# Top-k attention with an MLP behind it: two MLP pieces between two steps' scores, and an earlier place for the weights' transposing read

## The chip, the cores and the metric

One core of one Trainium2 chip runs the whole program. The metric is the device time of one execution in microseconds (us); lower is better. In the profile PE is TensorE's matrix multiply, PEld its weight load, DVE is VectorE, ACT is ScalarE, POOL is GpSimd, and SP is SyncE, which here only issues DMAs.

## What is computed

The attention takes 8 batches of 8 heads, 576 positions and 64 dimensions, and keeps the 32 largest scores of each row. Its output, as 4608 rows of 512, goes through a two-layer MLP.

```python
scores = scale * np.matmul(q, k.transpose(0, 1, 3, 2))
kth = np.partition(scores, -top_k, axis=-1)[..., -top_k:-top_k + 1]
scores = np.where(scores >= kth, scores, -1000000000.0)
attn = softmax(scores)                   # max subtracted, sum + 1e-09
x = np.matmul(attn, v)                   # then (B,H,S,D) -> (B*S, H*D)
h = x @ w_in                             # 4608x512 @ 512x2048
g = np.where(h >= 1, h, np.where(h <= -1, 0, (h + 1) ** 2 / 4))
out = g @ w_out                          # 2048x512
```

## The kernel before

**Steps.** The attention is cut into 144 steps (`n = len(steps)`). A step is one tile of 128 query rows for two heads; four steps make one chunk of 128 complete rows of x, and there are 36 chunks. Two batches share one chunk made of their last 64 rows. A step goes through these stages, which belong to different engines:

- `scores` (L349): matmuls on TensorE into two PSUM tiles `sp` (tag "a", 2 buffers), copied by ScalarE to `s` in two halves (L368). There are four `s` tiles.
- `weights` (L426) on VectorE: the search for the 32nd largest value (L381 to L460), then the masking of the exponentials `e` with their sum (L467). ScalarE makes `nmax` and `e` (L402, L404) from the first maxima. `divide` takes the reciprocal on VectorE (L413), and GpSimd scales `e` with it (L420), in the next step.
- `move_w` (L493): ScalarE splits `e` into 16-bit `halves` (L497), SyncE writes them to a DRAM tile `rows`, and a transposing DMA reads them back as `wT`. The read is put on the list `reads_of_rows` and issued later. Steps 0 to 7, and the last two, transpose on TensorE instead (`transpose_w`, L482).
- `values` (L506): `wT` with v on TensorE into `po` (tag "ph", 3 buffers), copied by ScalarE to `xT` (L527).

**The MLP in pieces.** When the fourth step of a chunk has its values, `mlp` (L538) adds 24 pieces to the queue `pending`. Eight are hidden pieces, called h0 to h7 here, of cost 8; sixteen are final pieces, f0 to f15, of cost 4; a chunk is 128 units. A hidden piece multiplies xT by w_in into a PSUM tile `ph` (tag "ph" too). Its `read` (L554) is two ScalarE activations, into `r` (2 buffers) and `g` (L558, L566), and its `bound` (L572) is three GpSimd instructions on r and g (L573, L575, L576). A final piece multiplies g by w_out into `py` (1 buffer); after f15, ScalarE copies `py` to `y` (L589) and SyncE stores it. The last eight final pieces of a chunk are marked, and are set among the next chunk's first hidden pieces.

**The order.** Everything is issued in the order of the program text (`manual_schedule`), so each engine's queue has that order. Each step of the loop (L801) has seven places (`slot` 0 to 6). The relevant ones are these:

- place 0: the first part of `weights`; the waiting transposing reads are issued.
- place 1: `queries(m + 5)` and one part of the next batch's key preparation. For batch 1 (`keys_of`, steps 8 to 11 here) a part is four TensorE transposes out of `k_in` (1 buffer), two ScalarE copies, and the load of the next `k_in`; at step 10 it also loads that batch's v. For later batches (`turned_keys_of`, at even steps) a part is a ScalarE copy into `parts` (L287), a write and a transposing read.
- place 2, at even steps: scores of step m + 2, then `issue_reads`, then the two values that are due (`values_until((m - 2) // 2 * 2)`), then scores of step m + 3.
- place 3: `inspect` at odd steps (L173: ScalarE looks at a `raw` piece of the MLP's weights, loaded by SyncE), `move_w` of step m - 1, then the loads that wait in `loads`.

At the end of each place `advance` takes pieces from `pending`. It keeps a credit, `due`:

```python
            due = due + amount if pending else 0.0
            pe_time = max(pe_time, until - 4.0)
            while pending and due >= pending[0][0] and pe_time < until and take():
                pass
```

`take` subtracts the piece's cost from `due` and adds it to `spent`. The amount per place is a seventh of `share`, which is what is left of the whole MLP over the steps left, but no more than what is pending over the steps until the next chunk comes.

In places 1 and 2 of even steps `holding` is set: the `read` of a hidden piece taken there is kept in the list `reads` and issued by `issue_reads` behind the scores of step m + 2. Anywhere else the read follows its matmuls at once:

```python
                reads.append(partial(read, x, ph))
                if not holding:
                    issue_reads()
```

Steps up to 7 are "early": the weights of the MLP are still being converted, and values are issued one step behind. At step 8 the loop issues values 7 with the old rule (L850), so at steps 8 and 10 no values are due in place 2; the first pair is values 8 and 9 at step 12.

Of the kernel before, what the change touches and what calls it, by code (L numbers as in the profile page):

```python
# [26 lines left out]
def kernel(  # L27
# [18 lines left out]
    NHP = H // 2  # L46
# [130 lines left out]
    def run(ctx, paired):  # L177
# [116 lines left out]
        def issue(x):  # L294
            while x:
                x.pop(0)()
# [235 lines left out]
        def rows_of(b, t):  # L532
            r0 = b * S
            if t < NT:
                return [(0, P, out[r0:r0 + SM, :].rearrange("(p c) n -> p c n", c=NT)[:, t, :])]
            return [(i * TL, (i + 1) * TL, out[r0 + i * S + SM:r0 + (i + 1) * S, :]) for i in range(2)]
# [110 lines left out]
        n = len(steps)  # L647
# [6 lines left out]
        pending = deque()  # L654
# [5 lines left out]
        def issue_reads():  # L660
            while reads:
                reads.pop(0)()
# [3 lines left out]
        def convert(time):  # L666

            nonlocal converted, begun
            while begun < min(converted + (2 if paired else 1), n_pieces):
                pipe.append(convert_piece(words, begun, not paired))  # L670
                next(pipe[-1])
                begun += 1
            next(pipe.popleft())
            converted += 1
            usable[converted] = time
            for i in range(begun, converted + (len(room) or 2)):
                load(words, i)
# [13 lines left out]
        def take():  # L691

            nonlocal spent, due, pe_time, taken
            cost, pieces, work, _ = pending[0]
            if pieces > converted or usable[pieces] > pe_time + 0.5:
                return False
            pending.popleft()
            due -= cost
            spent += cost
            pe_time += cost * UNIT_TIME  # L700
            work()
            taken = work.func
            return True

        def advance(amount, until):

            nonlocal due, pe_time
# [4 lines that stand above are left out]
            due = min(due, 24.0)  # L712
# [74 lines left out]
        next_keys, valued = 1, 0  # L787

        def values_until(m):
            nonlocal valued, pe_time  # L790
            while valued < min(m, n):
                pe_time = max(pe_time, ready_at[valued]) + 1.25
                values(state[valued])
                state[valued] = None
                if valued in ready:
                    ch = ready[valued]
                    mlp(xTs[ch], rows_of(*chunks[ch]), mlp_pool, ch == len(chunks) - 1)
                valued += 1

        first_late = None  # L800
        for m in range(n + 2):  # L801
            early = converted < n_pieces
            if not early and first_late is None:
                first_late = m
            elif not early and late is None:
                conversion.close()
                room.clear()
                late = ctx.enter_context(tc.tile_pool(name="late", bufs=1))

            share, left = (total - spent) / (n + 2 - m), sum(x[0] for x in pending)  # L810
            for r in sorted(ready):
                if r + 4 > m and r >= valued:
                    share = min(share, left / (r + 4 - m))
                    left += NK * NF + NF * DM // P
            top_k, parts = None, [0] * SLOTS
            if m < n:
                top_k = weights(state[m], state[m - 1] if m > 0 else None, state[m + 1] if m + 1 < n else None)
                parts = [1] * SLOTS if early else [1, 1, 0, 1, 1, 1, 1]
                start = max(dve_time, scored[m])
                now_converting = range(0, SLOTS, 2)  # L820
                dve_time = start + K_TIME + PIECE_TIME * min(len(now_converting), n_pieces - converted)
                done[m] = dve_time
                state[m]["by_tensor"] = early or m >= n - 2
            for slot in range(SLOTS):
                now = start + (dve_time - start) * (slot + 1) / SLOTS
                for _ in range(parts[slot]):
                    next(top_k, None)
                if slot == 0 or m >= n - 3:
                    issue(reads_of_rows)
                if m < n and converted < n_pieces:  # L830
                    if slot in now_converting:
                        convert(now)
                elif slot == 3 and late is not None:
                    if m % 2:
                        inspect()
                if slot == 1 and 1 <= m <= n and state[m - 1]["by_tensor"]:
                    pe_time = max(pe_time, done[m - 1] + 2.0) + 1.0
                    transpose_w(state[m - 1])
                    ready_at[m - 1] = pe_time + 1.8
                if slot == 3 and 1 <= m <= n and state[m - 1] is not None and not state[m - 1]["by_tensor"]:  # L840
                    move_w(state[m - 1])
                    ready_at[m - 1] = done[m - 1] + 15.0
                if slot == 1 and late is not None and paired and m % 2 == 0:
                    load(late, inspected, 1, 2)
                if slot == 3:
                    issue(turns)
                    issue(loads)
                if slot == SLOTS - 1 and m == n + 1 and paired:
                    judge(ps, att)
                if slot == 2 and (early or m == first_late or m >= n - 1):  # L850
                    values_until(m)
                if m == 0 and slot in (1, 2):
                    next(first)
                holding = not early and m % 2 == 0 and slot in (1, 2) and m < n
                if slot == 2 and not early:
                    if m % 2 == 0:
                        while len(reads) < 3 and pending and taken is not None and taken.__name__ == "hidden" and take():
                            pass
                    begin_until(min(m + 2, len(state)))
                    holding = False  # L860
                    issue_reads()
                    values_until((m - 2) // 2 * 2)
                    begin_until(m + 3 - m % 2)
                if slot == 4 and early:
                    begin_at(m + 2)
                if slot == (6 if early else 1):
                    queries(m + (3 if early else 5))
                    if (m < n and prep is None and next_keys < B and steps[m][0] == next_keys - 1 and steps[m][1] >= 1
                            and (next_keys > 1 or converted == n_pieces)):
                        prep = (turned_keys_of if next_keys > 1 else keys_of)(next_keys)  # L870
                    if prep is not None and (m % 2 == 0 or next_keys == 1):
                        got = next(prep, None)
                        pe_time += 0.5 if next_keys < 2 else 0.0
                        if got is None:
                            prep, next_keys = None, next_keys + 1
                        else:
                            keys[next_keys] = got
                            value_loads = got.get("loads", value_loads)
                    elif value_loads is not None:
                        loads.append(partial(next, value_loads, None))  # L880
                if paired and early and spent == 0 and not pending:
                    rest = ps.tile([P, NT, P], F32, name="rest", tag="py", bufs=1)
                    for i in range(5):
                        nc.tensor.transpose(rest[:, i % NT, :], ident, ident)  # L884
                advance((EARLY_SHARE if early else share) / SLOTS if m < n - 2 else 32.0, now)
                slots_done += 1
                while bounds and (early or m >= n or bounds[0][0] < slots_done - 2):
                    bounds.popleft()[1]()
            for _ in (top_k if top_k is not None else ()):
                pass  # L890
# [52 lines left out]
```

## Time and profile before

| what | value |
|---|---|
| median of 3 runs | 1472.83 us (1472.76 to 1473.66) |
| the profiled execution | 1471.88 us, its span 1470.1 us |
| mean granted TensorE clock | 0.992 |
| busy share of the span: PE, DVE, ACT, POOL | 97%, 95%, 79%, 63% |
| transposing reads of `rows` | 134, and as many writes of 576 KB, 3.2 us to landing |
| TensorE's scores of steps 18 and 142 start at | 196.41 and 1370.6 us |

The span is what the profiler saw from the first to the last instruction; the execution's own time is 1.8 us more. Busy shares are means over stages that differ. In the rows of groups and waits, a line such as L547 is the line of the code above, the count behind x is the number of instructions, and the name behind an arrow is what ended a wait.

### The profile page before, as it was taken

To read this page: it belongs to the slowest core of one execution; us is meant where nothing else is said; L and a number is where in the kernel's file an instruction comes from. 1 tells how busy PE (TensorE), PEld (TensorE's weight loads), DVE (VectorE), ACT (ScalarE), POOL (GpSimd) and SP (SyncE) were. 2 spreads that over 40 slices of the span, in tenths; PEclk is the share of its full clock that TensorE was granted. 3 is DMA by queue.
4 is the path that set the end of the run, shared out by engine and by line. 5 is a ranking of instruction groups with operands and counts; after the bars stand their busy time and mean duration, and the time that the engine had idled before them with its cause. 6 is when DMAs were issued, how large, how long until landed. Compare 5 with 4: busy or idle time off the path is not lost.

```text
span 1470.1 us, 32068 instructions
## 1 busy us (share of the span) xinstructions
PE 1433.2 (97%) x10787; PEld 1049.5 (71%) x10787; DVE 1395.7 (95%) x4392; ACT 1160.2 (79%) x2222; POOL 930.9 (63%) x1310
## 2 busy tenths in 40 slices
PE   6998899999999999999999999999999999999998
PEld 5776577777777777777777777777777777777777
DVE  6989999999999999999999999999999999999922
ACT  6986878888778888887778887888778888777642
POOL 3564577667666666666666666666666666666640
PEclk7999999999999999999999999999999999999999
DMA  7642766876778877886667797997667987665410
GB/s 233 199 133 57 201 161 183 217 188 165 164 177 211 217 200 192 210 218 177 173 168 204 207 216 177 224 215 181 174 165 187 224 214 175 167 163 151 137 41 17
DMA packets 508159, 260.42 MB, mean 177 GB/s; under 512 B 458704, under 2 KB 467152, under 8 KB 507984
## 3 DMA queue, kind: packets, MB, share of 16 engines
q1 hardware_dynamic: 507984, 258.27, 68.3%
q8 instruction: 87, 1.43, 0.4%
q14 instruction: 88, 0.72, 0.2%
HBM read 62.39 MB, written 102.63 MB: 112 GB/s over the span
## 4 chain that ended last, share of the span: by engine, by line
PE 91%; ACT 4%; DMA 2%; issue 1%; DVE 1%; SPq 1%; ACTq 0%
PE ph L547 34%; PE py L586 32%; PE sp L367 11%; PE po L514 10%; PE po L522 1%; PE pw L482 1%; DMA wT<-rows 1%; PE py_half L600 1%; ACT s L368 1%; ACT units L147 1%; ACT halves L497 1%; ACT wT L485 1%; ACT e L404 0%; DMA xT<-in_k_dram 0%; PE rest L884 0%
## 5 line engine op out<-in xcount | busy, mean ns | idle before, releaser
L547 PEld LDWEIGHTS ph<-xT,w_in 128*128 128x128 f32 x4608 | 547.0, 192 | 97.7 <-issue 66.8
L547 PE MATMUL ph<-xT,w_in 128*128 128x128 f32 x4608 | 555.6, 276 | 2.4 <-ACT g L566 1.8
L586 PE MATMUL py<-w_out,g 128*128 128x512 f32 x1120 | 526.6, 597 | 1.6 <-ACT y L589 1.6
L573 POOL TENSOR_SCALAR r<-r 128x256 f32<-128x256 f32 x280 | 138.3, 494 | 402.1 <-ACT r L558 397.9
L388 DVE MATCH_REPLACE8 more<-tops,more 128x288 f32<-128x288 f32 x864 | 379.1, 445 | 0.0
L420 POOL TENSOR_SCALAR e<-e,rz 128x576 f32<-128x576 f32 x268 | 304.3, 1145 | 12.6 <-DVE rz L413 12.6
L586 PEld LDWEIGHTS py<-w_out,g 128*128 128x128 f32 x1120 | 193.9, 191 | 164.9 <-issue 162.9
L497 ACT COPY halves<-e 128x1152 uint16<-128x1152 uint16 x268 | 293.8, 1144 | 0.0
L576 POOL TENSOR_TENSOR g<-r,g 128x256 f32<-128x256 f32 x280 | 233.4, 834 | 22.0
L467 DVE SCALAR_TENSOR_TENSOR e<-s,kth,e 128x577 f32<-128x577 f32 x288 | 242.9, 881 | 0.1
L404 ACT ACTIVATE e<-s,nmax 128x576 f32<-128x576 f32 x288 | 223.0, 775 | 4.7
L558 ACT ACTIVATE r<-ph,half 128x256 f32<-128x256 f32 (+1 forms) x296 | 136.9, 462 | 105.1 <-PE ph L547 100.5
L368 ACT ACTIVATE s<-sp 128x576 f32<-128x576 f32 x288 | 171.8, 650 | 43.2 <-PE sp L367 41.5
L575 POOL TENSOR_TENSOR r<-r 128x256 f32<-128x256 f32 x276 | 181.0, 656 | 23.0
L367 PE MATMUL sp<-kT,qT 64*128 64x288 f32 x1024 | 161.9, 434 | 4.8 <-ACT kT L265 3.4
L367 PEld LDWEIGHTS sp<-kT,qT 64*128 64x128 f32 x1024 | 89.8, 188 | 75.9 <-issue 30.5
L514 PE MATMUL po<-wT,v_in 128*64 128x128 f32 x2048 | 138.7, 276 | 4.9 <-DMA wT<-rows 4.1
L381 DVE TENSOR_TENSOR more<-s 128x576 f32<-128x576 f32 x144 | 134.7, 935 | 8.8 <-ACT s L368 8.8
L514 PEld LDWEIGHTS po<-wT,v_in 128*64 128x64 f32 x2048 | 113.4, 137 | 29.1 <-issue 12.2
L566 ACT ACTIVATE g<-ph,minus 128x256 f32<-128x256 f32 x280 | 130.8, 467 | 0.0
L429 DVE MAX8 tops<-more 128x8 f32<-128x288 f32 x288 | 125.9, 447 | 0.0
L437 DVE MAX8 tops<-more 128x8 f32<-128x288 f32 x288 | 117.0, 449 | 0.0
(95 smaller groups left out, 1370.1 us busy)
## 6 DMA issues: line engine op xcount, KB each, us to landing
rows<-halves SPq DMA_DIRECT2D x134, 576.0 KB, 3.2
lines<-parts SPq DMA_DIRECT2D x48, 256.0 KB, 3.3
q_in<-in_q_dram SPq DMA_DIRECT2D x32, 256.0 KB, 4.5
v_in<-in_v_dram SPq DMA_DIRECT2D x32, 256.0 KB, 4.0
raw<-in_moe_w_in_dram SPq DMA_DIRECT2D x32, 256.0 KB, 3.3
raw<-in_moe_w_out_dram SPq DMA_DIRECT2D x32, 256.0 KB, 3.2
out_dram<-y SPq DMA_DIRECT2D x31, 256.0 KB, 3.3
kT<-in_moe_w_in_dram SPq DMA_DIRECT2D x8, 512.0 KB, 4.5
```

Of the source, the lines that this page charges most:

```text
L367: nc.tensor.matmul(*x, start=True, stop=True)
L368: nc.scalar.activation(s[:, :, c0:c1], sp[:, :, 0:SH], AF.Copy, scale=SCALE)
L388: nc.vector.match_replace(out=st["rest"][:, i, :], in_to_replace=eight(st["tops"], i, r - 8), in_values=src[:, i, :], imm_value=LOWEST)
L404: nc.scalar.activation(e[:, i, :], s[:, i, :], AF.Exp, bias=nmax[:, i:i + 1])
L420: nc.gpsimd.tensor_scalar(st["e"][:, i, :], st["e"][:, i, :], rz[:, i:i + 1], 1.0, ALU.mult, ALU.mult)
L467: nc.vector.scalar_tensor_tensor(out=st["all"][1][:, i, :], in0=st["all"][0][:, i, :], scalar=last[i], in1=st["all"][1][:, i, :], op0=ALU. ...
L497: nc.scalar.copy(halves[:, :, i * S:(i + 1) * S], st["e"][:, i, :].bitcast(U16).rearrange("p (k t) -> p t k", t=2))
L514: nc.tensor.matmul(po[j * D:(j + 1) * D], v_in[:, h, c, :] if c < NT else tail_values(v_tl, h, t), wT[:, block(j, c)], start=(c == 0), sto ...
L547: nc.tensor.matmul(ph[:, i], w_in[:, kk, f * P:(f + 1) * P], xT[:, kk], start=(kk == 0), stop=(kk == NK - 1))
L575: nc.gpsimd.tensor_tensor(out=r, in0=r, in1=r, op=ALU.mult)
L576: nc.gpsimd.tensor_tensor(out=g, in0=r, in1=g, op=ALU.add)
L586: nc.tensor.matmul(py[0], gs[f // group][:, f % group], w_out[:, f, :], start=(f == 0), stop=(f == NF - 1))
```

## The change

It has two parts.

```diff
+        def fill(amount):
+            for _ in range(amount):
+                if pending:
+                    take()
+
...
-                if slot == 0 or m >= n - 3:
+                if slot == 0 or m >= n - 3 or slot == 5 and m < 4 * NHP:
                     issue(reads_of_rows)
...
                     begin_until(min(m + 2, len(state)))
                     holding = False
                     issue_reads()
+                    if valued >= (m - 2) // 2 * 2 and m % 2 == 0:
+                        fill(2)
                     values_until((m - 2) // 2 * 2)
                     begin_until(m + 3 - m % 2)
```

The first part: in place 2 of an even step, if the values that could be due there are already done, two pieces are taken from `pending` between the scores of step m + 2 and those of step m + 3. They are taken whatever the credit is; their cost goes from `due` all the same. With values issued as described above, the condition holds at steps 8, 10 and 144.

The second part: `NHP` is 4, so up to step 15 the transposing read of the step's `move_w` (place 3) is issued in place 5 of the same step, where before it was issued in place 0 of the next one. Since `move_w` starts with step 9, this concerns the reads of states 8 to 14.

## The prediction

> **What bounds the kernel now.** I read the page's busy shares, then busy time in stretches of 40 us, then the waits of TensorE, then SyncE's queue, then two steps instruction by instruction.
>
> ```profile
> PE 1433.2 (97%) x10787; PEld 1049.5 (71%) x10787; DVE 1395.7 (95%) x4392; ACT 1160.2 (79%) x2222; POOL 930.9 (63%) x1310
> ```
>
> In the stretches (columns: PE, PEld, DVE, ACT, POOL busy us) the gaps lie early:
>
> ```profile
> 120.00:160.00 40.00, 33.15 (x238) 23.98 (x236) 37.20 (x120) 30.27 (x62) 16.52 (x24) 0.96 0.42 122
> 160.00:200.00 40.00, 35.96 (x318) 27.11 (x322) 40.00 (x127) 32.30 (x63) 21.80 (x31) 1.00 0.69 183
> ...
> 1080.00:1120.00 40.00, 40.00 (x287) 28.99 (x286) 40.00 (x126) 30.88 (x61) 27.77 (x38) 1.00 0.64 168
> ```
>
> From 260 to 1400 us the list of waits holds none of TensorE's matmuls: four steps take it 37.77 us again and again. So TensorE sets the end; later than 260 us nothing is to be gained from it, and each new stall there is paid. TensorE's timeline shows the early gaps, in brackets with what ended them:
>
> ```profile
> 142.60 2.82 PE L547 MATMUL ph<-xT,w_in 128*128 128x128 f32 x16 [1.83 <-ACT g L566]
> ...
> 151.12 0.46 PE L341 MATMUL pq<-ident,q_tl 64*128 64x64 f32 x4 [1.25 <-ACT s L368]
> 152.38 0.63 PE L261 MATMUL pk<-ident,k_in 128*128 128x128 f32 x4 [0.80 <-DMA k_in<-in_k_dram]
> ...
> 162.45 1.09 PE L514 MATMUL po<-wT,v_in 128*64 128x128 f32 x16 [2.66 <-DMA wT<-rows]
> ...
> 195.39 1.10 PE L586 MATMUL py<-w_out,g 128*128 128x512 f32 x2 [1.60 <-ACT y L589]
> ```
>
> These are steps 10 to 16. SyncE's queue over steps 9 to 11:
>
> ```profile
> 141.18 0.35 SPq L499 DMA_DIRECT2D rows<-halves  x1
> 143.99 2.64 SPq L296 DMA_TRANSPOSE wT<-rows  x1
> 146.69 0.57 SPq L134 DMA_DIRECT2D raw<-in_moe_w_in_dram  x1
> 147.37 1.24 SPq L251 DMA_DIRECT2D k_in<-in_k_dram  x2
> ...
> 154.63 0.36 SPq L499 DMA_DIRECT2D rows<-halves  x1
> 157.87 2.40 SPq L296 DMA_TRANSPOSE wT<-rows  x1
> ```
>
> Each read starts 2.8 to 3.3 us behind its write, which is when the write lands. The read is not late because of its place.
>
> **What the skill says.** The Trainium skill, "PSUM — Partial Sum Buffer", Engine vs sequencer instructions: ScalarE's, VectorE's and GpSimd's queues are strict FIFO, and matmuls keep program order. The trace agrees: at 195.39 a ready y copy stood behind ScalarE's halves. "DMA: Bandwidth & Descriptors", Two DMAs through the same engine are not ordered: the issuer of a dependent DMA must wait for the first one's completion; the 2.8 us above are that. "SBUF — State Buffer", Who interferes with whom: VectorE instructions with two SBUF inputs contend with GpSimd's reads; L576 taking 0.73 us at one step and 1.88 at another fits.
>
> **The moved read: 0.** It concerns states 8 to 14. Between place 5 and the next place 0 SyncE gets only y stores, and none falls there in steps 9 to 15 (the one near, at 195.67, is issued in place 3). The order on SyncE stays; cover: the write's landing. If a store did stand between, it costs its 1.16 us on a read that has 5 us to spare: bounds -0.4 to 0.
>
> **The fill.** No values are due only at steps 8, 10 and 144. At 144 the two pieces come next anyway: 0. At step 8 it takes h0 and h1 of chunk 1 between scores 10 and 11; at step 10 it takes f0 and f1 between scores 12 and 13, and the credit keeps h2 back to step 10, place 1. No instruction is added; I follow the order with the durations of the rows (a hidden piece 1.78 us on TensorE, a final 0.86, scores 1.17, transposes of keys 0.5).
>
> Step 8 saves TensorE 0.27 + 0.21. But score copies of step 11 on ScalarE now wait for h1: they start at 135.3 instead of 131.8, and nmax and both e of step 9 behind them, so VectorE, whose L467 began at 136.0, begins at 137.4: +1.4 us for VectorE. On TensorE, key transposes 1 and 2 now have nothing between them (before: h0, h1, h2, 5.4 us). The key buffer is single: the load goes out after transpose 1 (136.7) and lands 3.2 us later, so TensorE idles 3.3. Behind that load SyncE has raw, for the weights' inspection, then the write of state 8; ScalarE copies halves only after the inspection. Write 8 goes from 141.2 to 144.6. Behind it SyncE has its read, raw, two key loads and eight value loads, 12.3 us without a pause to speak of; write 9 was issued 1.2 us after their end, so it moves 3.4 - 1.2 = 2.2 us, and with it the read that values 9 wait for: 162.45 becomes 164.7. On GpSimd the bounds of h0 and h1 now stand ahead of e of state 8, which moves from 126.2 to about 137.3; ScalarE asks for it at 142.4, so this costs nothing. At step 10 ScalarE has r and g of h2, h3, h4 together between the scores' copies, the third behind GpSimd's work on the first; copies 13 then end near 152, before write 9 can go. All pieces done before scores 15 are the same as before, so the other gaps disappear in this wait: **+2.2**. Later f15 comes one place earlier in step 15, ahead of step 16's nmax and halves 14: the y copy is in time, **-1.6**. Sum by step 16: **+0.6**; with 1.5 us for landings and for ScalarE's order either way, and at best all of the gaps gone, -8 to +3.
>
> **What it leaves behind.** Credit at the start of step 14 is what was paid in steps 9 to 13 less what was taken: before 110.07 - 108 = 2.07; after 18.67 + 22.4 + 20 + 22.67 + 24 - 104 = 3.73 (step 9 pays 112/6, as 16 of the 128 units are gone). From step 15 each place pays 4.57, four steps pay 128, one chunk, so 3.73 returns every four steps. At steps 16, 20, ..., 140: before, 2.07 + 4.57 = 6.64 < 8, h4 comes in place 1, where its read by ScalarE is held until the scores' copy (later carries up to 2.87 change nothing in this). After, 8.30 >= 8: h4 comes in **place 0, not held**. TensorE's order is the same as before from step 88 on. ScalarE's is not. Step 100 now:
>
> ```profile
> 992.26 0.45 ACT L558 ACTIVATE r<-ph,half 128x256 f32<-128x256 f32 x1
> ...
> 992.97 0.46 ACT L558 ACTIVATE r<-ph,half 128x256 f32<-128x256 f32 x1
> ...
> 993.68 1.04 ACT L287 COPY parts<-k_block 64x1024 uint16<-64x1024 uint16 x1
> 994.62 1.19 ACT L368 ACTIVATE s<-sp 128x576 f32<-128x576 f32 x2
> 995.69 0.48 ACT L558 ACTIVATE r<-ph,half 128x256 f32<-128x256 f32 x1
> ...
> 997.02 1.19 ACT L368 ACTIVATE s<-sp 128x576 f32<-128x576 f32 x2 [0.18 <-PE sp L367]
> ```
>
> The first two r are h2 and h3, the third is h4. r has two buffers, so h4's waits for GpSimd's last work on h2:
>
> ```profile
> 993.98 0.73 POOL L576 TENSOR_TENSOR g<-r,g 128x256 f32<-128x256 f32 x1
> ```
>
> Today that wait lies behind the scores' copy. After the change ScalarE stands at 993.7 until 994.7, then r and g of h4 (0.74), parts (0.94), and the scores' copy starts at 996.4 instead of 994.6. Its first half frees PSUM at 997.0; TensorE wants that bank at 996.2: a stall of 0.8. The same working at the other steps gives 1.2, 0.5, 0.3 (steps 20, 24, 28), 1.8 (44, 60, 64), 0.5 to 0.8 (48, 56, 80, 84, 92, 96, 116, 120), all with parts; without parts 0.95 at step 16, 0.8 at 40 and about 0 or less elsewhere (at 104, -0.1). One by one they sum to 15.4. They are not independent: ScalarE's chain there hangs on VectorE (nmax waits for tops 41 times between 260 and 1400), so a stall moves TensorE away from the next. TensorE's scores came 3.3 us behind VectorE's step at step 28, 1.35 at step 68: VectorE gives back 0.2 us in four steps, in its slow ones (38.2 against 37.77) 0.4. So stalls go on at 0.2 to 0.4 for each of 31 groups of four: 6 to 12; I take the middle less a little for the quiet start, **+8**. Bounds: 0 (ScalarE catches up) and 15.4.
>
> **Sum.** 0 + 0.6 + 8 = +8.6. The profiled execution took 1471.9 (span 1470.1): 1480.5. The median of the runs is 0.9 above it: 1481.4, said as 1481.
>
> **Rivals.** (a) *The gaps go and nothing comes back*: the stalls of step 8 and 10, the 1.83, the 1.25, the y wait: about -5, so 1468. It decides if write 9 does not move: that needs key load 2 to land before TensorE gets there, and h4's place to be harmless. For it: the gaps shown, 8.1 us, are real. Against: the key buffer is single and SyncE has 1.2 us of slack. (b) *The late stalls damp themselves*: after one stall of 0.8 to 1.8 TensorE stays far enough behind; then +0.6 + 1 = about 1474.5. For it: at steps 32 and 36, 2.7 to 2.9 us behind, the stall works out at 0. Against: VectorE drifted back from there by itself. (c) *L576 stays at 1.88 us* (as at steps 16 to 44) once TensorE lags more: every parts step wants 3.7 us of lag; nearly the whole 15.4, 1488. (d) The read's new place does act: within 0.4, no other case.
>
> **Numbers.** 0.2% is 2.9 us, about what a measurement of this kernel can tell from no change. Forecast and (c), slower by more: 0.65 (0.5 and 0.15). (b) and an early gain that meets a small late loss, within: 0.2. (a): 0.15. Slower alone would be 1476 to 1489. The range 1469.5 to 1489 leaves out most of (a) and the far end of (c), takes in (b), and follows the bounds.
>
> **What would show it.** Right: key transpose 2 with a wait on k_in near 140; values 9 with a wait on wT ending near 164.7; no wait on y near 195; r of h4 ahead of the scores' copy at steps 16, 20, ...; waits of TensorE's scores (L367) on ScalarE's s after 260 us, some 0.2 to 0.8 each and most in steps with parts; groups of four steps of 38 us where 37.77 stood. SyncE's pairs of write and read still 2.8 to 3.3 us apart. Wrong: no L367 waits after 260 us, or scores 18 starting 2 us or more ahead of 196.4.

## The result and the profile after

| | before | after |
|---|---|---|
| median of 5 runs, us | 1472.83 | 1487.66 (1487.3 to 1490.22) |
| ratio | 1 | 1.0107 (95% interval 1.0097 to 1.0118) |
| profiled span, us | 1470.1 | 1485.4 |
| start to scores 10 | 129.52 | 127.68 |
| scores 10 to scores 18 | 66.89 | 71.20 |
| scores 18 to scores 142 | 1174.19 | 1186.19 |
| scores 142 to the end | 99.50 | 100.33 |

The change makes the kernel 1.1% slower. The four stretches add up to the span's 15.3 us: 4.3 come at steps 10 to 18, 12.0 at steps 18 to 142, 0.8 at the end; the start, which the change does not touch, was 1.8 shorter in this execution (TensorE waited 2.90 us for a key load of the first batch where 4.58 stood). Over the kernels below the start takes 127.4 to 131.5 us. Below, steps 10 to 18 are "early", 18 to 142 "late".

The page's first part has TensorE busy 4.0 us longer than before (1433.2), so some 11 of the 15.3 us are waiting:

```profile
PE 1437.2 (97%) x10787; PEld 1051.5 (71%) x10787; DVE 1405.7 (95%) x4392; ACT 1155.4 (78%) x2222; POOL 914.7 (62%) x1310
```

The two stretches lose in different ways. Here is the early one, first before, then after (columns as in the prediction; the number behind POOL is the granted TensorE clock):

```profile
129.52:196.41 66.89, 58.01 (x436) 42.80 (x434) 64.86 (x206) 55.36 (x108) 33.25 (x49) 0.97 0.60 164
```

```profile
127.68:198.88 71.20, 62.27 (x437) 47.66 (x435) 65.67 (x205) 55.89 (x109) 35.00 (x52) 0.90 0.57 157
```

Early, TensorE is idle for 8.9 us in both, and its matmuls take 4.3 us longer at a lower clock: waits have moved, and rows behind them have become slower. Late, its idle time goes from 0.6 to 11.0 us, so there the loss is waiting.

**Early.** TensorE's timeline after (start, duration, group, and in brackets the idle time ahead with what ended it):

```profile
138.83 1.09 PE L261 MATMUL pk<-ident,k_in 128*128 128x128 f32 x4 [3.96 <-DMA k_in<-in_k_dram]
139.71 7.91 PE L547 MATMUL ph<-xT,w_in 128*128 128x128 f32 x48
...
165.15 1.98 PE L514 MATMUL po<-wT,v_in 128*64 128x128 f32 x16 [2.27 <-DMA wT<-rows]
...
167.48 1.77 PE L367 MATMUL sp<-kT,qT 64*128 64x288 f32 x8
...
197.93 1.02 PE L586 MATMUL py<-w_out,g 128*128 128x512 f32 x2
```

The predicted wait of key transpose 2 is there, and the wait on y near 195 is gone. But rows are longer that ought to be the same: h2 to h4 take 7.91 us where the 48 matmuls of h0 to h2 took 5.52 before, values 9 take 1.98 where 1.09 stood, and scores 15 take 1.77 where before has

```profile
163.69 1.24 PE L367 MATMUL sp<-kT,qT 64*128 64x288 f32 x8
```

Busy time in shorter stretches of the run after shows why (columns as above):

```profile
138.00:142.00 4.00, 3.17 (x15) 3.20 (x16) 4.00 (x15) 2.84 (x7) 1.63 (x3) 0.50 0.20 66
142.00:148.00 6.00, 6.00 (x43) 5.83 (x43) 6.00 (x21) 2.69 (x4) 0.00 (x0) 0.77 0.35 122
...
166.00:170.00 4.00, 4.00 (x31) 3.00 (x28) 4.00 (x15) 2.14 (x7) 1.01 (x2) 0.68 0.63 144
```

Behind the idle 3.96 us the clock is 0.50. ScalarE's and SyncE's rows of the same time:

```profile
152.70 0.47 ACT L558 ACTIVATE r<-ph,half 128x256 f32<-128x256 f32 x1 [1.71 <-POOL g L576]
...
153.43 1.19 ACT L368 ACTIVATE s<-sp 128x576 f32<-128x576 f32 x2
...
155.43 2.19 ACT L497 COPY halves<-e 128x1152 uint16<-128x1152 uint16 x2
```

```profile
142.88 0.35 SPq L499 DMA_DIRECT2D rows<-halves  x1
145.69 2.54 SPq L296 DMA_TRANSPOSE wT<-rows  x1
...
153.80 1.26 SPq L202 DMA_DIRECT2D v_tail<-in_v_dram  x2
157.64 0.36 SPq L499 DMA_DIRECT2D rows<-halves  x1
160.49 2.54 SPq L296 DMA_TRANSPOSE wT<-rows  x1
```

Write and read of a state stay 2.8 us apart. Write 9 leaves 2.6 us after the last value load ended: it waited for halves 9 on ScalarE, which stood behind the copies of scores 13, which stood behind the r of h4, which waited 1.71 us for its buffer.

**Late.** The waits from 260 to 1400 us (us in total, times, longest):

```profile
ACT s L368 <- PE sp L367: 59.4, 70, 3.2
...
ACT r L558 <- POOL g L576: 35.9, 31, 2.2
...
PE sp L367 <- ACT s L368: 10.6, 17, 1.6
...
ACT nmax L402 <- DVE tops L401: 0.8, 2, 0.4
```

The same two waits of ScalarE before, where TensorE's scores do not stand in the list at all:

```profile
ACT nmax L402 <- DVE tops L401: 41.2, 41, 1.6
...
ACT r L558 <- POOL g L576: 1.6, 4, 1.0
```

Step 100 after, ScalarE's rows first, then the rows of GpSimd and TensorE that it meets. The first row is r of h1, of the step before; from there to r of h4, at 1006.97, ScalarE has no idle time:

```profile
997.42 0.47 ACT L558 ACTIVATE r<-ph,half 128x256 f32<-128x256 f32 x1 [1.24 <-PE ph L547]
...
1004.50 0.45 ACT L558 ACTIVATE r<-ph,half 128x256 f32<-128x256 f32 x1
...
1006.97 0.47 ACT L558 ACTIVATE r<-ph,half 128x256 f32<-128x256 f32 x1 [0.94 <-POOL g L576]
...
1007.70 1.04 ACT L287 COPY parts<-k_block 64x1024 uint16<-64x1024 uint16 x1
1008.64 1.18 ACT L368 ACTIVATE s<-sp 128x576 f32<-128x576 f32 x2
```

```profile
1006.21 0.73 POOL L576 TENSOR_TENSOR g<-r,g 128x256 f32<-128x256 f32 x1
```

```profile
1009.34 1.29 PE L367 MATMUL sp<-kT,qT 64*128 64x288 f32 x8 [0.51 <-ACT s L368]
```

r of h4 now lies ahead of the scores' copy, waits for GpSimd's work on h2, and TensorE waits half a microsecond for the PSUM bank that the copy frees.

### The profile page after: what moved, and what is told of

It is laid out like the page before. It is cut to its first block, busy times and chain, and to the rows that moved or that the text cites. A ratio compares the mean times of both kernels' runs of the same rounds, so it can differ in the third digit from the quotient of the medians.

```text
span 1485.4 us, 32103 instructions
## 1 busy us (share of the span) xinstructions
PE 1437.2 (97%) x10787; PEld 1051.5 (71%) x10787; DVE 1405.7 (95%) x4392; ACT 1155.4 (78%) x2222; POOL 914.7 (62%) x1310
## 4 chain that ended last, share of the span: by engine, by line
PE 78%; ACT 13%; POOL 3%; issue 2%; DMA 2%; SPq 0%; DVE 0%; POOLq 0%; ACTq 0%
PE py L586 30%; PE ph L547 28%; PE sp L367 9%; PE po L514 7%; ACT halves L497 3%; ACT e L404 2%; ACT parts L287 2%; ACT s L368 1%; POOL g L576 1%; PE pw L482 1%; ACT r L558 1%; POOL r L575 1%; ACT g L566 1%; PE py_half L600 1%; ACT raw L173 1%
## 5 line engine op out<-in xcount | busy, mean ns | idle before, releaser
L573 POOL TENSOR_SCALAR r<-r 128x256 f32<-128x256 f32 x280 | 172.1, 615 | 445.6 <-ACT r L558 441.2
L388 DVE MATCH_REPLACE8 more<-tops,more 128x288 f32<-128x288 f32 x864 | 374.7, 437 | 0.0
L467 DVE SCALAR_TENSOR_TENSOR e<-s,kth,e 128x577 f32<-128x577 f32 x288 | 246.7, 892 | 3.6 <-ACT e L404 3.5
L576 POOL TENSOR_TENSOR g<-r,g 128x256 f32<-128x256 f32 x280 | 219.9, 785 | 22.0
L420 POOL TENSOR_SCALAR e<-e,rz 128x576 f32<-128x576 f32 x268 | 226.8, 856 | 1.8 <-DVE rz L413 1.2
L575 POOL TENSOR_TENSOR r<-r 128x256 f32<-128x256 f32 x276 | 184.0, 667 | 23.0
L367 PE MATMUL sp<-kT,qT 64*128 64x288 f32 x1024 | 162.1, 434 | 15.3 <-ACT s L368 11.0
L381 DVE TENSOR_TENSOR more<-s 128x576 f32<-128x576 f32 x144 | 126.2, 876 | 6.9 <-ACT s L368 6.9
```

The source lines that it names most:

```text
L367: nc.tensor.matmul(*x, start=True, stop=True)
L388: nc.vector.match_replace(out=st["rest"][:, i, :], in_to_replace=eight(st["tops"], i, r - 8), in_values=src[:, i, :], imm_value=LOWEST)
L420: nc.gpsimd.tensor_scalar(st["e"][:, i, :], st["e"][:, i, :], rz[:, i:i + 1], 1.0, ALU.mult, ALU.mult)
L467: nc.vector.scalar_tensor_tensor(out=st["all"][1][:, i, :], in0=st["all"][0][:, i, :], scalar=last[i], in1=st["all"][1][:, i, :], op0=ALU. ...
L575: nc.gpsimd.tensor_tensor(out=r, in0=r, in1=r, op=ALU.mult)
L576: nc.gpsimd.tensor_tensor(out=g, in0=r, in1=g, op=ALU.add)
```

## Experiments

**Theory.** Late: h4's read, no longer held, waits for one of the two r buffers in front of the scores' copy. Early: h0 and h1, taken at step 8, no longer lie between key transposes 1 and 2, so the single key buffer's load shows on TensorE and everything behind it on SyncE and ScalarE is late. **Rivals**: the read's new place; the early delay itself disturbing the later steps; for the early part, the pieces taken at step 10, or the granted clock.

All times in us; "early" is scores 10 to 18, "late" scores 18 to 142, in the profiled execution. Each ratio is to runs of the kernel before on the same chip.

| run | median | ratio (95% interval) | early | late |
|---|---|---|---|---|
| e1_fill_only | 1488.97 | 1.0110 (1.0093 to 1.0127) | 71.16 | 1186.37 |
| e2_read_only | 1471.79 | 1.0002 (0.9994 to 1.0011) | 67.07 | 1175.01 |
| e3_after_hold0 | 1472.42 | 1.0009 (1.0000 to 1.0017) | 70.69 | 1172.95 |
| e4_carry_only | 1482.65 | 1.0070 (1.0053 to 1.0086) | 66.77 | 1188.21 |
| e5_after_r3 | 1472.14 | 1.0007 (0.9996 to 1.0017) | 70.39 | 1172.95 |
| e6_hold0_keys | 1470.29 | 0.9997 (0.9988 to 1.0006) | 66.75 | 1172.95 |
| e7_hold0_warm | 1477.28 | 1.0036 (1.0021 to 1.0051) | 73.22 | 1173.06 |
| e7b_warm_gap | 1474.23 | 1.0016 (1.0007 to 1.0024) | 70.65 | 1172.95 |
| e8_hold0_fill8 | 1476.61 | 1.0041 (1.0027 to 1.0055) | 69.78 | 1177.19 |
| e9_hold0_fill10 | 1469.60 | 0.9991 (0.9981 to 1.0001) | 64.61 | 1174.73 |
| e10_carry_hold0 | 1468.57 | 0.9984 (0.9976 to 0.9992) | 64.21 | 1173.51 |
| e11_fill10_carry | 1470.27 | 0.9993 (0.9985 to 1.0002) | 66.52 | 1173.19 |

An early time has some spread of its own: e9 and e11, with the same order on every queue up to scores 17, reach scores 16 after 47.0 and 48.9 us. Without the pieces at step 8 the early time is 64.2 to 67.1 over five kernels and the one before. With the pieces at steps 8 and 10, and no other edit ahead of step 15 (after, e1, e3), it is 70.7 to 71.2.

### The two parts, each alone

e1_fill_only: the kernel before with the first part of the change alone.

```diff
+                    if valued >= (m - 2) // 2 * 2 and m % 2 == 0:
+                        fill(2)
```

> The change with the read's new place left out; every engine's queue holds the same instructions in the same order as with it. Theory: the read's place does nothing, so 1487.7 within 1 us, with the same waits. Rival (the new place matters): another time by 2 us or more.

e2_read_only: the second part alone.

```diff
-                if slot == 0 or m >= n - 3:
+                if slot == 0 or m >= n - 3 or slot == 5 and m < 4 * NHP:
```

> The kernel before with the moved reads alone; no piece is taken between the scores. Theory (each read waits for its write's landing, and no other transfer of SyncE lies between the two places): the same order on every queue, write and read 2.8 to 3.3 us apart as before, scores 10 to 18 between 64 and 67 us, 18 to 142 within 0.3 of 1174.2; ratio 0.999 to 1.001. Rival (the read's place does act, by letting values 9 start earlier or by holding something behind it on SyncE): reads more than 0.5 us nearer to their writes or further from them, ratio outside 0.998 to 1.002.

The fill alone is the whole loss, in both stretches; the read alone is nothing. e1's median lies 1.3 us above that of after, a little more than expected; in its profiled execution the start, where nothing differs, took 1.7 us longer. With the read alone, write and read of states 8 and 9 lie 2.8 and 3.3 us apart (140.59 to 143.41, 154.04 to 157.29), as before. Two of its numbers fell just outside what was expected: the early time by 0.1, and the late one by 0.5, with a wait of values on wT at 255.9 us of 1.27 where before has 0.48. It concerns a state whose read was not moved.

### The late loss: credit, place, buffer

e4_carry_only gives the kernel before the credit of the changed one, and nothing else. e3_after_hold0 leaves the change in and holds h4's read. e5_after_r3 leaves the change in, h4 unheld, and gives r a third buffer (at L557 and L611).

```diff
 e4:
+            due += 1.66 if m == 14 else 0.0
 e3:
-                holding = not early and m % 2 == 0 and slot in (1, 2) and m < n
+                holding = not early and m % 2 == 0 and slot in (0, 1, 2) and m < n
 e5:
     r: bufs=2 -> bufs=3
```

> The kernel before, with 1.66 added to the credit once, at the start of step 14; no fill, steps 8 to 13 untouched. Theory: the late loss comes back by itself: scores 18 to 142 take about 1186, the y wait of 1.6 at step 16 is gone; 1482 to 1484. Rival (early delay is the cause): 1471 to 1473.

> The change, but the read of a hidden piece is also held when the piece is taken in place 0 of an even step. Theory (the credit moves h4 to place 0, where its read goes ahead of the scores' copy on ScalarE): the waits of the scores' matmuls (10.6 us between 260 and 1400) vanish, four steps take 37.8 us again, scores 18 to scores 142 take 1174 us as before instead of 1186; 1475 to 1477. Rival (the late loss is a lasting effect of the early delay, VectorE and TensorE out of step): 1486 to 1488.

> The change with three buffers for r instead of two; order unchanged. Theory (what makes ScalarE stand is the wait for the buffer of r that GpSimd still reads): ScalarE's waits of r for L576 (35.9 us) vanish; the scores' copy at step 100 starts near 0.74 us later than before the change, not 1.8, and TensorE's wait goes: 1475 to 1478. Rival (the order alone, two more activations ahead of the copy, is enough): most of the 12 us stays, 1484 or more.

e4 has the late loss without any early delay (1188.21; its scores wait 11.6 us, its r 35.3). e3 and e5 take it away by different means, and both arrive at 1172.95 us to the hundredth. The waits of e3 in the same stretch as above:

```profile
ACT nmax L402 <- DVE tops L401: 48.7, 55, 2.3
```

TensorE's scores no longer stand in the list; nmax waits for tops again. So the early delay does not cause the late loss, and place 0 costs only through r's buffer. Both are some 3 us faster than expected: the late stretch is shorter than before's own, and before itself ran at 1470.79 beside them, not at 1472.83. Against e3, the unheld h4 costs 1186.19 - 1172.95 = 13.24 us. e3 gains 1.24 on before, mostly in steps 22 to 26 (38.5 us where 39.2 stood); how much of that is the credit's is open, since e2, whose late order is that of before, differs from it by 0.8.

Scores to scores over four steps, after less e3, says where the 13.24 fell: 0.5 to 1.7 in each group from scores 22 to 54 (7.0 in all), then 0.5 to 0.7 in each group whose scores' copy has `parts` ahead of it, and 0.0 in the others.

### The early loss: step 8 or step 10

Both hold place 0, so the late loss is out.

```diff
 e8:
+                    if m == 8:
+                        fill(2)
 e9:
+                    if m == 10:
+                        fill(2)
```

> The changed kernel with place 0 held, and the two pieces taken at step 8 alone (not at 10 and 144). Theory (taking h0 and h1 out from between key transposes 1 and 2 is what costs): key transpose 2 waits near 3.8 us, and scores 10 to 18 takes 69 to 71 us, nearly all of the 70.7. Rival (the two finals taken at step 10, and h2 to h4 packed behind them on ScalarE, cost it): the wait at 138 is there, but 10 to 18 is 66 to 68.

> The changed kernel with place 0 held, and the two pieces taken at step 10 alone (not at 8 and 144). Theory (step 8 is what costs): key transpose 2 finds its keys there within 0.5 us, as before, and scores 10 to 18 takes 65 to 67 us; time 1467 to 1470, since from scores 18 to 142 the held place 0 takes 1172.95, 1.2 less than before. Rival (step 10 costs): 10 to 18 is 69 to 71; time 1471 to 1473.

Step 8 is what costs (69.78, with a wait of 3.92 us at key transpose 2); the two finals at step 10 cost nothing that shows (64.61). In e9, e10 and e11 the held place 0 does one thing more: at step 10 it holds h2, and f0, which stood ahead of scores 12, comes behind them. At step 10 they differ from the kernel before by this too. Neither e8 nor e9 keeps the late 1172.95: their credit at step 14 is 1.73 and 2.40, so h4 comes in place 1. e8's late time is 3.0 above that of before, mostly in steps 46 to 66; the cause of that stays open.

### The early loss: key buffer, clock or ScalarE's order

e6_hold0_keys is e3 with the third pair of keys in the space of `k_tl`, loaded before the second pair is transposed, and the fourth pair loaded before the third is (its line numbers are 2 higher). e7b_warm_gap is e3 with 20 transposes of the identity in the idle time; e7_hold0_warm was the first try.

```diff
 e6:
+                elif hp == 2:
+                    k_in = stage.tile([P, NT, 2, D], F32, name="k_in2", tag="k_tl", bufs=1)
...
-                k_next = load_keys(hp + 1) if hp + 1 < NHP and b == 0 else None
+                k_next = load_keys(hp + 1) if hp + 1 < NHP and (b == 0 or hp in (1, 2)) else None
...
 e7, e7b:
+                if m == 9 and slot == 1:      # e7b: slot == 2
+                    rest = ps.tile([P, NT, P], F32, name="rest", tag="py", bufs=1)
+                    for i in range(20):
+                        nc.tensor.transpose(rest[:, i % NT, :], ident, ident)
```

> The changed kernel with place 0 held (so the late loss is out: 1172.95 us from scores 18 to scores 142), and with a second buffer for chunk 1's third pair of keys (the space of k_tl), loaded before the second pair is transposed and not after it. Theory (the early loss is TensorE's idle time for the single key buffer, and the slow clock and late queues that follow it): key transpose 2 no longer waits 3.8 us, h2 to h4 take about 5.5 us and not 7.9, and scores 10 to scores 18 takes 66 to 68 us against 70.7; time about 1468 to 1470. Rival (the order on ScalarE, h0 and h1 ahead of the copies of scores 11 and h2 to h4 between those of step 10, costs the time whatever the keys do): the wait goes, but another takes its place before scores 15, and 10 to 18 stays at 70 to 71; time 1472.

> The changed kernel with place 0 held, and 20 transposes of the identity (their result is used by nothing) put on TensorE between key transposes 1 and 2, where it idles 3.8 us. They add some 2.5 us of work inside that gap and change no wait. Theory (a part of the early loss is the lower clock granted after the idle time): the granted clock from 138 to 148 us rises from 0.5 to 0.8 toward 1.0, h2 to h4 take 5.5 to 6.5 us and not 7.9, scores 10 to 18 falls from 70.7 to 68 to 69.5; time 1470 to 1471. Rival (the clock does not depend on the gap, or the waits that follow absorb it: values 9 wait for their read whatever h2 to h4 take): 10 to 18 stays at 70.5 to 71; time 1472 to 1473.

> As e7_hold0_warm, with the 20 transposes (2.4 us) one place later, so that they lie behind key transpose 1, in the idle 3.9 us itself, and not ahead of it. Theory (the clock granted after the idle time is a part of the early loss): key transpose 2 starts when it did (within 0.3 us), the clock from 138 to 148 us is 0.9 or more where 0.50 and 0.77 stood, h2 to h4 take about 5.5 us, and scores 10 to 18 takes 68.5 to 69.7 us against 70.7. Rival (what h2 to h4 lose is taken up by the waits behind them): h2 to h4 are as short, but 10 to 18 stays at 70.3 to 71, since values 9 wait for their read the longer. Third: the clock does not depend on the gap, and h2 to h4 stay above 6.6 us.

e7 put its transposes ahead of key transpose 1, not behind it: the idle time stayed (3.94) and began later. The stretch grew by 2.5 us, which is what the 20 transposes take (2.40). So e7 says nothing on the clock, but it suggests that the chain from key transpose 1 on has no slack: what is put ahead of it is paid in full.

e7b fills the gap. TensorE's timeline there:

```profile
138.48 2.35 PE L874 MATMUL rest<-ident 128*128 128x128 f32 x20
142.42 0.63 PE L261 MATMUL pk<-ident,k_in 128*128 128x128 f32 x4 [1.59 <-DMA k_in<-in_k_dram]
142.88 5.52 PE L547 MATMUL ph<-xT,w_in 128*128 128x128 f32 x48
...
168.41 1.32 PE L514 MATMUL po<-wT,v_in 128*64 128x128 f32 x16 [2.55 <-DMA wT<-rows]
```

The 48 matmuls of h2 to h4 take 5.52 us and the clock from 138 to 148 us is 1.00, so their 7.91 and 6.63 (after, e3) are the clock that follows the idle time. Yet the stretch stays at 70.65, and values 9 still wait 2.55 us for their read, as the rival of that run said. This one execution is not a clean measure, though: from the issue of read 9 to values 9 it took 6.1 us, where the other runs show 4.4 to 4.8. The medians are the better evidence: e7b's ratio is 1.0016 over 20 executions, e3's 1.0009 over 12, so filling the gap gained nothing that shows.

e6 removes the wait itself, and with it most of the early loss: 66.75. Scores 16 come 1.7 us later than before, where e3 has 5.7; waits of 2.10 us on ScalarE's key copies at scores 12 and of 2.07 us on the next keys stand there now. What is gained between scores 16 and 18, where the y wait was, covers the 1.7. ScalarE's order is the same as in e3, and its r of h4 waits longer than in after (1.94 against 1.71), so that order alone does not make the larger part. Times after the start of scores 10:

| | before | after | e5 | e7b | e6 |
|---|---|---|---|---|---|
| write 8 | 11.66 | 15.20 | 15.04 | 15.05 | 13.98 |
| write 9 | 25.11 | 29.96 | 27.16 | 27.13 | 26.33 |
| values 9 | 32.93 | 37.47 | 35.76 | 36.97 | 34.65 |
| scores 15 done | 35.34 | 41.51 | 40.31 | 40.87 | 37.06 |
| scores 16 | 46.56 | 52.73 | 51.92 | 52.19 | 48.29 |
| scores 18 | 66.89 | 71.20 | 70.39 | 70.65 | 66.75 |

Two routes lead to write 9, side by side. In e5 (no wait for r) and e7b (full clock ahead of it) write 9 leaves within 0.1 us of the end of SyncE's value loads: +2.0. In after, ScalarE's route ends last: +4.85. That size is one execution's: in e1, with the same order on every queue, r of h4 waits 0.93 us and not 1.71, write 9 comes +2.85 and values 9 +3.4, and scores 16 start as late as in after (52.70). Take one route away, and most of the loss stays: the other holds write 9, and behind the wait for read 9 values 9 and scores 15 run slowly (4.6 us in e5 and 3.9 in e7b, for 2.4 before). Only the key buffer's wait is ahead of both routes.

### Versions for use

e10_carry_hold0 is the kernel before with e3's line and the credit of e4; e11_fill10_carry is e9 with 1.33 of credit at step 14.

> The kernel before with the credit of the changed kernel (1.66 added at step 14) and place 0 held; no piece is taken between the scores and no read is moved. Theory (the credit's only harm is that h4's read is not held; what it puts earlier is a gain): no wait of TensorE on s after 260 us, 1172.95 us from scores 18 to 142 (1.2 less than before), 65 to 67 us from scores 10 to 18, time 1469 to 1471.5, ratio 0.998 to 0.9995. Rival (the credit costs on its own): 18 to 142 above 1175, time above 1474.

> The two pieces taken at step 10 alone, place 0 held, and 1.33 of credit added at step 14, so that the credit is 3.73 as in the changed kernel. Theory: the 64.6 us of e9_hold0_fill10 from scores 10 to 18 and the 1172.95 us of e3_after_hold0 from 18 to 142 come together: some 3.5 us less than before, time about 1467 to 1469.5, ratio 0.9965 to 0.999. Rival (64.6 was the luck of one execution, or the gain is given back later): ratio 0.999 to 1.001.

e10 beats both kernels: 1468.57, 0.16% below before, with an interval that excludes 1; no wait of TensorE on s after 260 us. It was better early than expected (64.21) and 0.6 worse late. The early gain lies between scores 16 and 18 (17.60 us where 20.33 stood; e4, with the same added credit, has 17.61). e11 missed: its early time is 66.52, not 64.6, with a wait of 3.31 us ahead of values 9 and those at 1.97 us; e9 and e11 differ by 1.9 us ahead of scores 16, where their order is the same, so the 64.61 of e9 was in good part that execution's.

## Why the prediction was right, and where it was not

The forecast was slower, 1481 (1469.5 to 1489); the median is 1487.66. The mechanism was right, and both terms of the sum were too small. The median lies inside the range by 1.3 us, and two of the five executions (1490.05 and 1490.22) lie outside.

- **The moved read, 0**: right. e2 measures 1.0002, and the distances of write and read did not change.
- **h4 in place 0 from the credit of 3.73**: right. e4, which has nothing but that credit, shows it.
- **Late, +8, measured +12.0.** The step that failed is "a stall moves TensorE away from the next", with VectorE giving back 0.2 to 0.4 in each of 31 groups. Nothing had to be given back. TensorE does come to lie further behind VectorE's step (4.3 to 5.0 us where 1.2 to 1.35 stood), and nmax stops waiting for tops (0.8 us in all). But from then on ScalarE's chain hangs on TensorE itself, as the rows of step 100 show: h1's matmuls, r of h1, ScalarE's queue without a pause to r of h2, GpSimd's L576, r of h4, parts, the copy, and back to TensorE's scores. A stall that is measured from TensorE's own earlier work does not shrink when TensorE is late. So from scores 54 on every group with parts pays 0.5 to 0.7 for good, 18 of the 31 groups pay something, and the others pay nothing. The prediction's stalls without damping were close in sum (15.4 against 13.2), and the steps that pay from step 56 on are those it listed, with step 100 that it showed; the damping laid over them was the error. That the sums are so close is in part luck: the stalls at steps 60 and 64 were 0.6 each and not 1.8, and steps 24 to 36, put at 0.5, 0.3 and about 0, cost 0.5 to 1.1 each. The discount "for the quiet start" was on the wrong end too: scores 22 to 54 brought 7.0 of the 13.2.
- **Rival (c)** came nearest in size (15.4) by a wrong mechanism: L576 did not stay at 1.88 us. Its mean is 0.78 us from 260 to 1400, and one of 238 lies above 1.3. **Rival (b)**, stalls that damp themselves, is what the profile excludes; **(a)** failed as said there, since write 9 moved.
- **Early, +0.6, measured +4.3.** Write 8 was right (+3.4 predicted, +3.54 measured), and the y gain too (-1.6 predicted; between scores 16 and 18 the changed kernel is 1.86 shorter). "+2.2" for write 9 was mis-sized, because "copies 13 then end near 152, before write 9 can go" was wrong: they ended at 154.6, in an execution that had reached scores 10 1.8 earlier, by way of the slow h2 to h4 and the 1.71 us for r's buffer, and write 9 came +4.85, values 9 +4.5. ScalarE's route had no slack to begin with: before, halves 9 ended at 154.60 and write 9 left at 154.63. The 2.2 is the right size of SyncE's route, as e5 and e7b show.
- **The missing term**: the granted clock. Values 9 and scores 15 together take 4.0 us after, 4.6 in e5, 3.9 in e7b, and 2.4 in before and in e6. That is +1.6 behind values 9 (+2.2 in e1), which nothing takes back. Behind key transpose 2 it is 2.4 more; filling that gap gained nothing that shows (e7b), but in after this time lies on ScalarE's route to write 9, so how much of it counted there is open. The Trainium skill has it: "TensorE: Matmul & The Clock Gate", Part 1: The HAM clock gate, says that the array runs at half its clock after an idle window of about 3.4 us. The prediction put 3.3 us of idle time ahead of key transpose 2, lengthened the wait of values 9 as well, and kept the durations of a TensorE at full clock. Its own row of h4, 2.82 us behind a wait of 1.83 where 16 such matmuls take 1.95, had shown the clock falling.
- **The ends of the range**: the bounds of the early term (-8 to +3) did not hold the 4.3; those of the late one (0 to 15.4) did.

## What to carry to other kernels

When a piece of work is moved out from between two users of a single buffer, what it covered was the buffer's load: look for the next load of that buffer before counting the gain in front. When an order has a credit or a budget, follow a change of it through the whole run, to the first place where a piece crosses into one with other rules. And ask of a predicted stall what it is measured from: if its chain begins on the engine that stalls, being late does not cure it, and it recurs as long as the order does.

## What was unexpected on the hardware

The clock can fall after less idle time than one window of the page named above, and stay up after nearly as much. In before, h4 waited 1.83 us and took 2.82, and the clock from 144 to 146 us was 0.50; in e9 the same matmuls waited 1.88 us and took 2.05, at a clock of 1.00. In e6, waits of 0.80 and 2.07 us close together were enough for h5 to take 3.62 us where 1.95 is usual. Values 9 took 1.09 us in e2 behind 3.32 us of idle time, and 1.97 in e11 behind 3.31. Behind the early waits of 3.8 us and more the rows were slow in every run. So between 1.8 and 3.3 us of idle time it is a matter of the execution, and it goes with the spread of the early stretch: e9 and e11, one order up to scores 17, come to scores 16 1.9 us apart, and in e11 scores 15 took 2.29 us, in e9 1.24.
